# Chunked delta attention and two Mlps on one core: weights signed by ScalarE's Prelu and read where they are converted, group 0's keys first, each group prepared a stage earlier

## The chip, the core and the metric

The kernel runs on one core of a Trainium2 chip. A core has TensorE (PE, with its weight load shown apart as PEld), VectorE (DVE), ScalarE (ACT), GpSimd (POOL) and SyncE (SP, which here issues nearly all transfers), each with an instruction queue worked off in order, and 16 DMA engines. The metric is device time in microseconds (us) per execution, lower is better.

## The reference

```python
k_n = k / (norm(k) + 1e-6)                       # q, k, v: 4 x 8 heads x 768 steps x 48
for t in range(768):
    y[:, :, t] = q_t @ state                     # state 48 x 48 per head
    state += beta_t * outer(kn_t, v_t - state^T kn_t)
x = y as (3072, 384)
h = x @ w_in; P = a0 + a1 h + a2 h^2 + a3 h^3; Q = 1 + |b0||h| + |b1|h^2
x = (P / (Q + 1e-6)) @ w_out                     # Mlp1, 384 -> 2048 -> 384
h = x @ w2_in; out = (h * tanh(softplus(h))) @ w2_out    # Mlp2
```

The four weight matrices arrive as 64-bit floats, passed as integer words. The rest is fp32.

## The kernel before

**Attention.** 768 steps are 24 chunks of 32 (C); four chunks (GU) are a group of 512 columns, six groups. `norms` takes the squares of the keys (ACT), sums (DVE) and roots. `prepare`, per chunk: scale the keys (POOL, L332), a masked beta (`mb`, POOL, L337), transpose keys and queries on PE (L309), copy them to the slot `kq` (ACT, L313), one gram matmul for both (L321), mask its two parts (DVE, L327). `inverse`, per group: a transpose (L357), 30 elimination steps of two instructions each (L366, L372; on POOL for groups 1 to 5, on DVE for group 0), a transpose back (DVE, L376) and a scaling by beta of 1024 columns into `xt` (POOL, L379). `step`, per chunk: the state applied to the keys (L421), its rest `r` (L427), W, the inverse applied to `r` (L433), `u` (L439), the new state S in two halves of 32 matmuls each (L450, L458), then Y, its copy and the transposed X (L469 to L494), which is the Mlp's input. The swapped keys `kns` (L414, L415) are transfers from SBUF to SBUF that S reads.

**Mlps.** Each works group by group in 16 units of 128 hidden columns. A unit is 9 matmuls of 512 columns up (L641), the activation, and 9 down (L647; 12 of 384 columns in the last group's Mlp2, L656): fp32 is carried as two parts, hi and lo, hence three products. A unit fetches its two weight tiles `win` and `wout` from a DRAM scratch `wd` (L634), into 4 slots.

**Weights.** 64 tiles of 128x384 (2 Mlps, 16 f, 2 sides) are converted from 64-bit to fp32 words: raw words by DMA into one of 3 buffers, magnitude by ACT's Abs (L551; on DVE for 20 tiles, L549), a clamp (L554), shift (L559), sign bits (L564) and low bits (L569) on DVE, hi by ACT (L576), lo by POOL (L579), and a store to `wd` (L592).

**What sets the order.** Everything is added to a `Plan` with the engine, an estimated duration, the buffers read and written, and sometimes a due time. `order` simulates the engines and picks, on each, the ready work with the earliest latest start; that makes the fixed order of every queue. Its estimates only choose the order. `heat` matmuls (L787) fill PE's pauses of the head. The stages after the head are: Mlp1 and Mlp2 of group 0, of 1, of 2, of 3 (the steps of group g+1 beside Mlp2 of g, the preparation of g+2 beside Mlp1 of g+1), then Mlp1 of 4, Mlp1 of 5, Mlp2 of 4, Mlp2 of 5.

## Time and profile before

| | |
|---|---|
| median of 3 runs | 1348.69 us (1339.13 to 1351.46) |
| profiled execution, its span | 1342.18 us, 1340.5 us |
| PE, PEld busy | 1098.8 (82%), 873.9 (65%) |
| DVE, ACT, POOL busy | 713.5 (53%), 586.1 (44%), 570.8 (43%) |
| moved by DMA | 224.79 MB, mean 168 GB/s |
| first up matmul of each stage | 113.3, 264.6, 409.6, 500.8, 597.5, 685.2, 786.4, 879.4, 983.0, 1113.0, 1178.7, 1244.0 |

Busy time is the union of an engine's instructions; PE's ends are modelled. In the stage table (Rows 1) a row is a stretch: its bounds, its length, then for PE, PEld, DVE, ACT and POOL the busy us and number of instructions, the mean clock granted to TensorE as a share of full speed, the busy share of the DMA engines, and GB/s. In a group of instructions the columns are line, engine, operation, output and input with shapes, count, then busy us in all and mean ns, then idle us just before them with what ended it. In a timeline they are start, length, engine, line, operation, and in brackets the idle time before with its releaser.

### The profile page before, as it was taken

The page shows a single profiled execution, that of the slowest core. Times are in us where ns is not written, and L with a number is a line of the kernel's source. Part 1 is how long each engine was busy: PE and PEld are TensorE (multiplying, and loading weights), DVE is VectorE, ACT ScalarE, POOL GpSimd, SP SyncE. Part 2 cuts the span into 40 slices and gives each one's busy share as a digit, 9 for nine tenths or more (in the row PEclk, how much of TensorE's full clock was granted, in tenths as well). Part 3 has the DMA queues.
Part 4 walks back from the last instruction along what each step waited for, and adds up shares of the span by engine and source line. Part 5 has one row for each costly group of instructions (what it writes and reads, how often), then busy time and mean ns, then how long its engine had stood idle before and what let it go on. Part 6 is the DMA issues. An engine that isn't in the chain of part 4 may idle for free.

```text
span 1340.5 us, 32163 instructions
## 1 busy us (share of the span) xinstructions
PE 1098.8 (82%) x13168; PEld 873.9 (65%) x13168; DVE 713.5 (53%) x1172; ACT 586.1 (44%) x1022; POOL 570.8 (43%) x699
## 2 busy tenths in 40 slices
...
GB/s 100 116 164 175 240 255 244 205 237 222 263 284 165 174 188 163 136 144 105 243 171 108 141 142 115 231 165 97 126 127 104 80 125 166 195 194 191 151 194 64
DMA packets 209283, 224.79 MB, mean 168 GB/s; under 512 B 134864, under 2 KB 147664, under 8 KB 209136
## 3 DMA queue, kind: packets, MB, share of 16 engines
...
q8 instruction: 104, 1.70, 0.5%
...
q0 software_dynamic: 256, 0.10, 0.0%
...
## 4 chain that ended last, share of the span: by engine, by line
PE 45%; POOL 10%; DVE 9%; DMA 6%; SPq 6%; ACT 5%; issue 3%; DVEq 0%; POOLq 0%; ACTq 0%
PE b_h L641 18%; PE b_o L647 17%; SPq L719 4%; POOL xs L372 4%; POOL tmp L366 3%; PE b_t L450 3%; PE b_t L469 2%; DMA wd<-st 2%; DMA win<-wd 2%; DMA raw<-in_moe_w_in_dram 1%; PE b_t L433 1%; PE b_o L656 1%; POOL gh L687 1%; DVE b_r L684 1%; DMA out_dram<-ev 1%
## 5 line engine op out<-in xcount | busy, mean ns | idle before, releaser
L641 PE MATMUL b_h<-x,win 128*128 128x512 f32 x1728 | 461.5, 415 | 79.2 <-DVE ms L680 42.6
L647 PE MATMUL b_o<-gh,wout 128*128 128x512 f32 x1584 | 417.8, 411 | 66.2 <-POOL gh L687 41.4
L641 PEld LDWEIGHTS b_h<-x,win 128*128 128x128 f32 x1728 | 334.6, 198 | 165.0 <-DVE ms L680 50.8
L647 PEld LDWEIGHTS b_o<-gh,wout 128*128 128x128 f32 x1584 | 302.7, 196 | 145.2 <-POOL gh L687 49.2
L689 ACT ACTIVATE gh<-b_h 128x512 fp32r<-128x512 f32 x96 | 57.4, 598 | 272.3 <-PE b_h L641 266.7
L691 DVE TENSOR_TENSOR gh<-mq,gh 128x512 fp32r<-128x512 f32 x96 | 69.5, 728 | 179.9 <-ACT mq L690 177.2
L678 POOL TENSOR_TENSOR mq<-mq,mr 128x512 f32<-128x512 f32 x96 | 125.6, 1308 | 87.6 <-ACT mr L676 80.0
L687 POOL TENSOR_TENSOR gh<-mq,gh 128x512 fp32r<-128x512 f32 x96 | 125.1, 1304 | 65.2 <-ACT gh L686 51.0
L579 POOL TENSOR_TENSOR st<-wm,st 128x384 fp32r<-128x384 f32 x64 | 68.5, 1077 | 119.6 <-ACT st L576 100.2
L337 POOL TENSOR_TENSOR mb<-beta_t,mask 128x256 f32<-128x256 f32 x24 | 16.6, 690 | 241.4 <-DVE lg L327 241.2
L683 DVE SCALAR_TENSOR_TENSOR mq<-mq,b_r 128x512 f32<-128x512 f32 x96 | 65.4, 682 | 59.6 <-ACT b_r L682 57.0
L672 ACT ACTIVATE mq<-b_h 128x512 f32<-128x512 f32 x96 | 57.0, 593 | 90.8 <-PE b_h L641 64.0
L679 DVE TENSOR_TENSOR ms<-ms,b_h 128x512 f32<-128x512 f32 x96 | 65.2, 679 | 47.4 <-ACT ms L677 46.8
L372 POOL TENSOR_TENSOR xs<-xs,tmp 128x30 f32<-128x30 f32 (+9 forms) x150 | 82.0, 547 | 11.8
L670 ACT ACTIVATE mr<-mq,cst 128x512 f32<-128x512 f32 x96 | 69.1, 721 | 29.1 <-POOL mq L678 28.8
L366 POOL TENSOR_TENSOR tmp<-xs 128x30 f32<-128x30 f32 (+9 forms) x150 | 77.6, 518 | 8.6
L677 ACT ACTIVATE ms<-b_h,ab 128x512 f32<-128x512 f32 x96 | 73.9, 770 | 0.6 <-PE b_h L641 0.6
L680 DVE SCALAR_TENSOR_TENSOR ms<-ms,ab,b_h 128x512 f32<-128x512 f32 x96 | 71.2, 742 | 1.7
L684 DVE SCALAR_TENSOR_TENSOR b_r<-ms,ab,b_r 128x512 f32<-128x512 f32 x96 | 71.8, 748 | 0.0
L682 ACT ACTIVATE b_r<-mr 128x512 f32<-128x512 f32 x96 | 57.5, 599 | 28.8 <-DVE mq L685 27.7
L576 ACT CAST st<-wm 128x384 fp32r<-128x384 f32 x64 | 32.3, 509 | 80.4 <-DVE wm L569 48.6
L686 ACT CAST gh<-mq 128x512 fp32r<-128x512 f32 x96 | 58.7, 612 | 19.3 <-DVE mq L685 19.0
(124 smaller groups left out, 1350.0 us busy)
## 6 DMA issues: line engine op xcount, KB each, us to landing
win<-wd SPq DMA_DIRECT2D x192, 384.0 KB
wout<-wd SPq DMA_DIRECT2D x192, 384.0 KB
...
v<-in_v_dram SPq DMA_DIRECT2D x192, 24.0 KB
...
```

The costliest lines, as they stand in the source:

```text
L366: eng.tensor_tensor(out=tv, in0=xs[:, j, j + 1:C].unsqueeze(1).to_broadcast([128, j, n]), in1=xs[:, 0:j, j:j + 1].to_broadcast([128, j, n] ...
L372: eng.tensor_tensor(out=xs[:, 0:j, j + 1:C], in0=xs[:, 0:j, j + 1:C], in1=tv, op=ALU.add)
L579: nc.gpsimd.tensor_tensor(out=st[:, 1], in0=mf, in1=st[:, 0].bitcast(F32), op=ALU.subtract)
L641: nc.tensor.matmul(out=h, lhsT=win[:, a, j], rhs=x[:, c, slab[j]], start=n == 0, stop=n == 8)
L647: nc.tensor.matmul(out=self.banks[f"o{d}"], lhsT=wout[:, a, d], rhs=gh[:, c], start=first and j == 0, stop=last and j == 2,)
L670: act(out=r, in_=q, func=ACTF.Ln, bias=k["c"])
L677: p.add("ACT", 775, lambda: act(out=s, in_=h, func=ACTF.Identity, scale=k["a3"], bias=k["a2"]), [hb], [sb])
L678: p.add("POOL", 1335, lambda: P.tensor_tensor(out=q, in0=q, in1=r, op=ALU.mult), [rb], [qb])
L680: p.add("DVE", 750, lambda: V.scalar_tensor_tensor(out=s, in0=s, scalar=k["a1"], in1=h, op0=ALU.add, op1=ALU.mult), [hb], [sb])
L684: p.add("DVE", 750, lambda: V.scalar_tensor_tensor(out=rp, in0=s, scalar=k["a0"], in1=rp, op0=ALU.add, op1=ALU.mult), [sb], ["r"])
L687: p.add("POOL", 1320, lambda: P.tensor_tensor(out=gh[:, 1], in0=q, in1=gh[:, 0].bitcast(F32), op=ALU.subtract), [qb], [ghb])
L691: p.add("DVE", 755, lambda: V.tensor_tensor(out=gh[:, 1], in0=q, in1=gh[:, 0].bitcast(F32), op=ALU.subtract), [qb], [ghb])
```

## The change

Weights: one clamp with both signs, then Prelu with a negative slope puts the sign in place (tiles of Mlp1, and of f 0 to 3 of Mlp2), or a scale and a maximum (the other 24 tiles); shift and low bits follow. 24 tiles, all in the head, are clamped on POOL and get their lo by two matmuls with the identity and its negative, and a copy; the others are clamped on DVE and get lo by POOL as before. The split is written to the slot of `win` or `wout` (8 slots for group 0, four of them in the space of the later Mlp inputs), and group 0 reads it there, except for units 8 to 11; it is stored to `wd` as before. The raw buffers are five.

Attention: group 0 does keys, inverse and scaling before its queries, its inverse lies in PSUM, its state copies run on ACT. Later three more `kq` slots take the space of the raw words. S is one operation over both halves, `xt` is scaled chunk by chunk. Group g+3 is prepared beside Mlp2 of g and Mlp1 of g+1, and the steps of group 5 run beside Mlp1 of group 4. The planner's own costs change too.

```diff
-EARLY = 6
-RAW = 3
+HEAD = 12
+FETCHED = range(8, 12)
+EARLY = 4
+RAW = 5
 WM = 3
+SWITCH = 150
+NEAR = 20000
+SIGNS = ""
+PACE1 = 6500
...
+    NT, NKN, NQ, NV, NX = 5, 8, 2, 2, 3
+    WIDE = 12
...
+    def slot(self, u):
+        return u % self.NT if u < self.WIDE else (5, 6, 7, 2, 3, 4, 0, 1)[(u - self.WIDE) % 8]
+    def qslot(self, u):
+        return u if u < GU else u % self.NQ
...
+        for u in range(GU):
+            self.load_k(u, nc.sync, (0, 1))
+            self.load_k(u, nc.scalar, (2, 3))
...
+        for what in ("k", "q") if G == 0 else ("kq",):
+            for g in range(GU):
+                self.prepare(p, GU * G + g, what)
+            if "k" in what:
+                self.inverse(p, G)
+            if what == "k":
+                self.finish(p, G)
+                p.add("DVE", 980, lambda: self.nc.vector.memset(self.pair, 0.0), (), ["o0", "o1"])
...
+            on, eng, ns = ("DVE", nc.vector, 480) if u in (0, 2) else ("POOL", nc.gpsimd, 840)
...
+    def solved(self, G):
+        return (self.xs, ["xs"]) if G else (self.pair.rearrange("p (a b) -> p a b", a=C), ["o0", "o1"])
...
+            if G == 0 and j in (1, half):
+                rows = slice(0, half) if j == 1 else slice(half, C)
+                p.add("ACT", 400 if j == 1 else 800, lambda rows=rows: nc.scalar.copy(out=row[:, rows], in_=xs[:, rows]), xb, ["xs"], early=lead(AHEADX, G))
...
+        def scale(g):
+            part = xt[:, g * M:g * M + M]
+            beta = self.beta_t[:, GU * G + g].unsqueeze(2).to_broadcast([128, M, C])
+            return lambda: eng.tensor_tensor(out=part, in0=part, in1=beta, op=ALU.mult)
...
-        def s_mm(c):
-            s_ps = self.banks[bs[c]]
-            def f():
-                for m in range(M):
-                    a, n = divmod(m, 4)
-                    for e in (c, 2 + c):
-                        r = self.srow(e)
-                        rows = slice(32 * e, 32 * e + 32)
-                        nc.tensor.matmul(
-                            out=s_ps[r:r + 64, m * D:(m + 1) * D],
-                            lhsT=kn[rows, 2 * n + r // 64, :] if a == e // 2 else kns[rows, n, :],
-                            rhs=U[rows, m, :], start=True, stop=True,
-                        )
-            return f
+        def s_mm():
+            for m in range(M):
+                a, n = divmod(m, 4)
+                for e in (0, 3, 1, 2):
+                    r = self.srow(e)
+                    rows = slice(32 * e, 32 * e + 32)
+                    nc.tensor.matmul(
+                        out=self.banks[bs[e % 2]][r:r + 64, m * D:(m + 1) * D],
+                        lhsT=kn[rows, 2 * n + r // 64, :] if a == e // 2 else kns[rows, n, :],
+                        rhs=U[rows, m, :], start=G > 0, stop=True, skip_group_check=G == 0,
+                    )
+        def s_copy(c):
+            return lambda: nc.scalar.copy(out=T[:, c].rearrange("p m d -> p (m d)"), in_=self.banks[bs[c]][:, 0:M * D])
...
+        at, to = (pv, v) if "v" in kind else (v, pv)
...
-        def mag():
-            if late:
-                nc.vector.tensor_scalar(out=m, in0=words[:, :, 1], scalar1=0x7FFFFFFF, scalar2=None, op0=ALU.bitwise_and)
-            else:
-                nc.scalar.activation(out=m.bitcast(F32), in_=words[:, :, 1].bitcast(F32), func=ACTF.Abs)
-        def size():
-            nc.vector.tensor_scalar(
-                out=m.bitcast(F32), in0=m.bitcast(F32), scalar1=self.LEAST, scalar2=self.MOST, op0=ALU.max, op1=ALU.min,
-            )
+        def clamp():
+            (nc.vector if "v" in kind else nc.gpsimd).tensor_scalar(
+                out=at, in0=high.bitcast(F32), scalar1=self.MOST, scalar2=-self.MOST, op0=ALU.min, op1=ALU.max,
+            )
+        def fold():
+            nc.scalar.activation(out=at, in_=at, func=ACTF.Prelu, scale=self.DOWN, alpha=self.SIGN)
+        def scale():
+            nc.scalar.activation(out=to, in_=at, func=ACTF.Identity, scale=self.DOWN)
+        def sign():
+            nc.vector.scalar_tensor_tensor(out=pv, in0=at, scalar=self.SIGN * self.DOWN, in1=to, op0=ALU.mult, op1=ALU.max)
         def shift():
             nc.vector.tensor_scalar(
-                out=m, in0=m, scalar1=3, scalar2=0x3FFFFFF8, op0=ALU.logical_shift_left, op1=ALU.bitwise_and,
-            )
-        def sign():
+                out=ps, in0=ps if kind else m, scalar1=3, scalar2=None, op0=ALU.logical_shift_left,
+            )
+        def tail():
             nc.vector.scalar_tensor_tensor(
-                out=m, in0=words[:, :, 1], scalar=-(1 << 30), in1=m, op0=ALU.bitwise_and, op1=ALU.bitwise_or,
-            )
-        def low():
-            nc.vector.scalar_tensor_tensor(
-                out=m, in0=words[:, :, 0], scalar=29, in1=m, op0=ALU.logical_shift_right, op1=ALU.bitwise_or,
+                out=m, in0=low, scalar=29, in1=ps, op0=ALU.logical_shift_right, op1=ALU.bitwise_or,
             )
...
-            nc.scalar.copy(out=st[:, 0], in_=mf)
+            nc.scalar.copy(out=split[:, 0], in_=mf)
...
+        rest = self.banks["h1"][:, 0:384]
+        def lo_mm():
+            nc.tensor.matmul(out=rest, lhsT=self.ident, rhs=v, start=True, stop=False)
+            nc.tensor.matmul(out=rest, lhsT=self.minus, rhs=split[:, 0].rearrange("p k c -> p (k c)"), start=False, stop=True)
+        def lo_copy():
+            nc.scalar.copy(out=split[:, 1].rearrange("p k c -> p (k c)"), in_=rest)
...
+        here, there = (bank, mb) if "v" in kind else (mb, bank)
+        if "v" in kind:
+            p.add("DVE", 520, clamp, [rawb], [here])
+        else:
+            p.add("POOL", 1490, clamp, [rawb], [here])
         if late:
-            p.add("DVE", 400, mag, [rawb], [mb])
+            p.add("ACT", 550, scale, [here], [there])
+            p.add("DVE", 580, sign, [mb], [bank])
+            p.add("DVE", 470, shift, (), [bank])
         else:
-            p.add("ACT", 550, mag, [rawb, "table"], [mb])
-        p.add("DVE", 400, size, (), [mb])
-        p.add("DVE", 430, shift, (), [mb])
-        p.add("DVE", 640, sign, [rawb], [mb])
-        p.add("DVE", 640, low, [rawb], [mb])
-        p.add("ACT", 510, hi, [mb], [stb])
-        p.add("POOL", 1060, lo, [mb], [stb])
-        p.dma(380, 384, lambda: nc.sync.dma_start(out=self.scratch[f][:, side], in_=st.bitcast(F32)), [stb], [f"wd{self.n}_{f}_{side}"])
+            p.add("ACT", 550, fold, ["table"], [here])
+            p.add("DVE", 470, shift, [here], [bank])
+        p.add("DVE", 550, tail, [rawb, bank], [mb])
+        p.add("ACT", 510, hi, [mb], [buf])
+        if "v" not in kind:
+            p.add("PE", 1000, lo_mm, [mb, buf], ["h1"], early=3000)
+            p.add("ACT", 520, lo_copy, ["h1"], [buf])
+        else:
+            p.add("POOL", 1060, lo, [mb], [buf])
...
+    def wslot(self, i, nf):
+        NW = self.NW
+        if i < nf:
+            return ((0, 1, 2, 3, 4, 5, 6, 7) * 2)[i]
+        if i < 2 * nf:
+            return ((0, 1, 2, 3, 6, 7) * 3)[i - nf]
+        return i % NW
...
+            if i in FETCHED:
...
+        if G or i in FETCHED:
+            p.dma(330, 384, fetch(0, win), [f"wd{m - 1}_{f}_0"], [winb], early=6000)
+            p.dma(330, 384, fetch(1, wout), [f"wd{m - 1}_{f}_1"], [woutb], early=6000)
...
+    def units(m, g, host, convert=lambda f: None):
+        nonlocal due
         for f in range(NF):
+            convert(f)
+            ml.plan_unit(plan, m, g, NG, f, NF, due)
+            due += (PACE if due > START + NF * PACE1 - 1 else PACE1) + HOST * host
+    def first(f):
+        for n in range(HEAD if f == 0 else 0):
+            ml.convert(plan, 1, n, "r", NF, SIGNS)
+        if 0 <= f - 5 < NF - HEAD:
+            ml.convert(plan, 1, HEAD + f - 5, "t1", NF, SIGNS + "v")
+        if 0 <= f - 12 < EARLY:
+            ml.convert(plan, 2, f - 12, "t1", NF, SIGNS + "v")
+    def second(f):
+        for n in (range(EARLY, 6) if f == 0 else (f + 5,)):
+            if n < NF:
+                ml.convert(plan, 2, n, "r", NF, "mv")
+    def prepare(g):
+        at.norms(plan, g)
+        at.prepares(plan, g)
+    units(1, 0, 0, first)
+    at.prepares(plan, 1)
+    at.finish(plan, 1)
+    at.norms(plan, 2)
+    for g in range(NG - 2):
+        at.steps(plan, g + 1)
+        units(2, g, 1, second if g == 0 else lambda f: None)
+        if g == 0:
+            at.prepares(plan, 2)
+        at.finish(plan, g + 2)
+        if g + 3 < NG:
+            at.norms(plan, g + 3)
+            at.prepares(plan, g + 3)
         else:
+            at.steps(plan, g + 2)
+        units(1, g + 1, g + 2 == NG - 1)
+    units(1, NG - 1, 0)
+    units(2, NG - 2, 0)
+    units(2, NG - 1, 0)
```

Three places in the queues, as they stand in the two programs. First POOL, the end of the elimination of the last group (`xs`, `tmp`), with the products of Mlp1 of group 4 behind it (`mq`, `mr`, `gh`). Before:

```order
L372 TENSOR_TENSOR xs_155<-xs_155,tmp_157 128x29x2
L366 TENSOR_TENSOR tmp_157<-xs_155 128x30
L372 TENSOR_TENSOR xs_155<-xs_155,tmp_157 128x30
L687 TENSOR_TENSOR gh_194<-mq_186,gh_194 128x512
L687 TENSOR_TENSOR gh_195<-mq_187,gh_195 128x512
L379 TENSOR_TENSOR xt_156<-xt_156,beta_t_123 128x1024
L674 TENSOR_SCALAR mr_192<-mq_185,ab 128x512
L678 TENSOR_TENSOR mq_185<-mq_185,mr_192 128x512
```

And now:

```order
L425 TENSOR_TENSOR xs_172<-xs_172,tmp_174 128x29x2
L419 TENSOR_TENSOR tmp_174<-xs_172 128x30
L425 TENSOR_TENSOR xs_172<-xs_172,tmp_174 128x30
L449 TENSOR_TENSOR xt_173<-xt_173,beta_t_146 128x256 x4
L798 TENSOR_TENSOR mq_123<-mq_123,mr_132 128x512
L794 TENSOR_SCALAR mr_130<-mq_124,ab 128x512
```

The products `gh` of Mlp1 no longer stand between the elimination and its scale; the Mlp1 work that comes behind the scale begins with its first product.

Second SP, in the head: raw weights (`raw`, now in `arena`), keys of group 1 (`kn`), the swap of the fourth chunk's keys (`kns`), stores to and fetches from the scratch (`wd`). Before:

```order
L192 DMA kn_125<-in_k_dram 32x8x48 x4
...
L545 DMA raw_111<-in_moe_w_in_dram 48x128
L592 DMA wd_1_61<-st_116 128x768
L534 DMA raw_109<-in_moe_w_out_dram 128x384
L414 DMA kns_137<-kn_127 64x4x48
L415 DMA kns_137<-kn_127 64x4x48
L634 DMA win_177<-wd_1_61 128x768
L634 DMA win_178<-wd_2_62 128x768
```

And now:

```order
L610 DMA arena<-in_moe_w_out_dram 128x384
L229 DMA kn_147<-in_k_dram 32x8x48 x4
L617 DMA arena<-in_moe_w_in_dram 48x2x128 x2
...
L477 DMA kns_153<-kn_147 64x4x48
L478 DMA kns_153<-kn_147 64x4x48
L684 DMA wd_5_65<-x_113 128x768
```

The swap stands behind more raw loads (196 transfers of SP are ahead of its second half), no fetch follows it, and the store is from the place where the unit reads.

Third DVE, in Mlp1 of group 0: conversion between the units' own work (`ms`, `mq`, `b_r`). Before:

```order
L679 TENSOR_TENSOR ms_189<-ms_189,b_h_99 128x512
L554 TENSOR_SCALAR wm_114<-wm_114 128x384
L559 TENSOR_SCALAR wm_114<-wm_114 128x384
L554 TENSOR_SCALAR wm_113<-wm_113 128x384
L559 TENSOR_SCALAR wm_113<-wm_113 128x384
L564 SCALAR_TENSOR_TENSOR wm_113<-raw_110,wm_113 128x384
L569 SCALAR_TENSOR_TENSOR wm_113<-raw_110,wm_113 128x384
L564 SCALAR_TENSOR_TENSOR wm_114<-raw_111,wm_114 128x384
L569 SCALAR_TENSOR_TENSOR wm_114<-raw_111,wm_114 128x384
L683 SCALAR_TENSOR_TENSOR mq_186<-mq_186,b_r 128x512
```

And now:

```order
L624 TENSOR_SCALAR b_t_103<-arena 128x384
L799 TENSOR_TENSOR ms_128<-ms_128,b_h_99 128x512
L800 SCALAR_TENSOR_TENSOR ms_128<-ms_128,ab,b_h_99 128x512
L638 TENSOR_SCALAR b_t_103<-b_t_103 128x384
L643 SCALAR_TENSOR_TENSOR arena<-arena,b_t_103 128x384
L803 SCALAR_TENSOR_TENSOR mq_124<-mq_124,b_r 128x512
```

A tile has three instructions on DVE instead of four or five, and its shift and low bits read PSUM.

## Rows read from the trace of the kernel before

**Rows 1.** The stage table: stretches between first up matmuls, and the head.

```profile
0.00:113.30 113.30, 61.94 (x1760) 54.76 (x1760) 68.87 (x161) 28.63 (x59) 30.77 (x60) 0.74 0.55 129
113.30:264.60 151.30, 97.14 (x571) 69.43 (x568) 133.78 (x198) 83.96 (x154) 92.08 (x92) 0.82 0.76 231
264.60:409.60 145.00, 108.93 (x1742) 83.07 (x1742) 98.73 (x178) 48.71 (x91) 61.59 (x75) 0.87 0.81 252
409.60:500.80 91.20, 79.62 (x443) 62.73 (x443) 62.75 (x96) 61.10 (x99) 70.51 (x85) 0.94 0.61 170
500.80:597.50 96.70, 93.68 (x1602) 73.95 (x1601) 26.77 (x42) 27.93 (x53) 14.83 (x25) 0.98 0.57 145
...
983.00:1113.00 130.00, 98.82 (x1737) 76.13 (x1736) 66.30 (x102) 63.01 (x104) 78.59 (x103) 0.88 0.39 105
1113.00:1178.70 65.70, 65.52 (x289) 53.95 (x288) 53.09 (x80) 52.71 (x89) 43.33 (x38) 1.00 0.69 188
...
1244.00:1340.50 96.50, 76.25 (x364) 67.87 (x362) 14.31 (x21) 18.47 (x34) 0.00 (x0) 0.92 0.47 134
```

**Rows 2.** SP's timeline from the start; first and last of 101 issues.

```profile
0.81 4.59 SPq L192 DMA_DIRECT2D kn<-in_k_dram  x8
...
56.96 0.43 SPq L634 DMA_DIRECT2D wout<-wd  x1
```

**Rows 3.** TensorE's timeline at its three longest pauses after 409.6 us.

```profile
713.24 1.50 PE L433 MATMUL b_t<-r,xt 32*32 32x48 f32 x64 [6.90 <-POOL xt L379]
...
907.20 1.50 PE L433 MATMUL b_t<-r,xt 32*32 32x48 f32 x64 [6.68 <-POOL xt L379]
...
1046.47 6.19 PE L647 MATMUL b_o<-gh,wout 128*128 128x512 f32 x16 [27.00 <-POOL gh L687]
```

**Rows 4.** Groups of instructions by form: conversion of weights, POOL's one-input operation.

```profile
L579 POOL TENSOR_TENSOR st<-wm,st 128x384 fp32r<-128x384 f32 x64 | 68.5, 1077 | 119.6 <-ACT st L576 100.2 <-ACT nrm L279 14.8 <-issue 3.7
...
L569 DVE SCALAR_TENSOR_TENSOR wm<-raw,wm 128x384 int32<-128x384 int32 x64 | 47.5, 748 | 1.6
...
L674 POOL TENSOR_SCALAR mr<-mq,ab 128x512 f32<-128x512 f32 x48 | 38.3, 797 | 32.4 <-ACT mq L672 32.3
L554 DVE TENSOR_SCALAR wm<-wm 128x384 f32<-128x384 f32 x64 | 36.5, 570 | 19.7 <-ACT wm L551 18.9
L559 DVE TENSOR_SCALAR wm<-wm 128x384 int32<-128x384 int32 x64 | 32.5, 507 | 2.0
...
L549 DVE TENSOR_SCALAR wm<-raw 128x384 int32<-128x384 int32 x20 | 10.2, 512 | 13.4 <-DMA raw<-in_moe_w_in_dram 6.6 <-POOL st L579 4.2 <-DMA raw<-in_moe_w_out_dram 2.6
```

**Rows 5.** The page's costliest groups: elimination on POOL, five groups.

```profile
L372 POOL TENSOR_TENSOR xs<-xs,tmp 128x30 f32<-128x30 f32 (+9 forms) x150 | 82.0, 547 | 11.8
...
L366 POOL TENSOR_TENSOR tmp<-xs 128x30 f32<-128x30 f32 (+9 forms) x150 | 77.6, 518 | 8.6
```

**Rows 6.** The timeline of all engines, 61 to 68 us.

```profile
61.38 2.01 DVE L376 STREAM_TRANSPOSE xt<-xs 128x1024 f32<-128x1024 f32 x1
...
63.47 1.91 POOL L379 TENSOR_TENSOR xt<-xt,beta_t 128x1024 f32<-128x1024 f32 x1 [24.41 <-DVE xt L376]
63.59 2.00 DVE L554 TENSOR_SCALAR wm<-wm 128x384 f32<-128x384 f32 x1
...
66.61 0.56 DVE L569 SCALAR_TENSOR_TENSOR wm<-raw,wm 128x384 int32<-128x384 int32 x1
```

**Rows 7.** TensorE's timeline, 521 to 530 us: W, a unit, half an S.

```profile
521.85 0.88 PE L433 MATMUL b_t<-r,xt 32*32 32x48 f32 x64
522.66 2.35 PE L641 MATMUL b_h<-x,win 128*128 128x512 f32 x9
524.94 0.25 PE L450 MATMUL b_t<-u,kn 32*64 32x48 f32 x1
...
526.01 2.35 PE L647 MATMUL b_o<-gh,wout 128*128 128x512 f32 x9
```

**Rows 8.** SP's waits: engine, line, waited for, us in total, times, longest.

```profile
SPq L592 <- POOL st L579: 20.7, 14, 6.8
```

More of the change, by code (lines that the diff above doesn't have):

```diff
@@ L104, in order @@
             end = t + self.ops[i][1]
+            if engine == "PE":
+                wide = self.ops[i][1] > 2000
+                end += SWITCH if wide and not was else 0
+                was = wide
             free[engine] = end
@@ L112, in order, with run @@
         return done
-    def run(self, idle, unit, until):
+    def run(self, idle, unit):
         last, fill = None, True
@@ L119, in run @@
             if engine == "PE":
-                fill = fill and i < until
+                fill = fill and ns <= 2000
                 if last is not None and fill:
@@ L185, in bank, with load_k @@
         if u < GU:
-            of = {"t": ("t1", "h0", "h1"), "c": ("t0",), "s": ("o0", "o1"), "y": ("o2",), "x": ("h1",)}[what]
+            of = {"t": ("t1", "h0"), "c": ("t0",), "s": ("o0", "o1"), "y": ("o2",), "x": ("t1",)}[what]
             return of[n % len(of)]
-        return "t1" if what in "tx" else "t0"
-    def load_k(self, u, engine=None):
-        for e in range(4):
+        if u < 2 * GU and what == "t":
+            return "t0"
+        return "t1" if what in "tx" or what == "s" and n else "t0"
+    def load_k(self, u, engine=None, es=range(4)):
+        for e in es:
             (engine or self.nc.sync).dma_start(
@@ new lines, in prepare @@
+        if "q" in what:
+            p.dma(4 * 450, 300, lambda: self.load_q(u), (), [qnb], early=lead(AHEADP, G))
+            p.add("PE", 600, transpose(qn, tq), [qnb], [tq], early=lead(AHEADP, G))
+            p.add("ACT", 580, copy(tq, 1), [tq], [qb] + taken, early=lead(AHEADX, G))
+        p.add("PE", 1100, gram, [kb] + ([qb] if "q" in what else []), [tg], early=lead(AHEADP, G))
+        if "k" in what:
+            p.add("DVE", 430, part(self.lg[:, g], 0, mb), [tg, mbb], [f"lg{g}"], early=lead(AHEADX, G))
@@ L352, in inverse @@
+        if "q" in what:
+            mask_a = self.mask_a.unsqueeze(1).to_broadcast([128, M, C])
+            p.add("DVE", 430, part(am, 1, mask_a), [tg], [ab] + taken, early=lead(AHEADX, G))
+    def solved(self, G):
+        return (self.xs, ["xs"]) if G else (self.pair.rearrange("p (a b) -> p a b", a=C), ["o0", "o1"])
     def inverse(self, p, G):
-        nc, M, tmp, xt, xs = self.nc, self.M, self.tmp, self.xt, self.xs
+        nc, tmp = self.nc, self.tmp
+        xs, xb = self.solved(G)
+        row, half = self.xs, 8
@@ L522, in __init__, with plan @@
+    SIGN = -(2.0 ** 32)
+    def __init__(self, nc, n, w_in, w_out, raw, wm, banks, scratch):
+        self.nc, self.n, self.scratch = nc, n, scratch
+        self.raw, self.wm, self.banks = raw, wm, banks
         self.w_in = w_in
         self.w_out = w_out.rearrange("f (k c) -> f k c", c=128)
-    def plan(self, p, f, side, j, late):
-        nc, bufs = self.nc, self.bufs
-        raw, m, st = (bufs[n][j % len(bufs[n])] for n in ("raw", "wm", "st"))
-        rawb, mb, stb = (f"{n}{j % len(bufs[n])}" for n in ("raw", "wm", "st"))
+    def plan(self, p, f, side, j, bank, split, buf, kind):
+        late = "m" in kind
+        nc = self.nc
+        raw, m = self.raw[j % len(self.raw)], self.wm[j % len(self.wm)]
+        rawb, mb = f"raw{j % len(self.raw)}", f"wm{j % len(self.wm)}"
@@ L615, in __init__, with convert @@
         self.ev = ring("ev", 2, [128, TOK])
-        self.n = 0
+        self.n = self.nst = 0
+    def wslot(self, i, nf):
[5 more added lines that the diff above has]
+        return i % NW
+    def convert(self, p, m, f, bank, nf, kind):
+        i = (m - 1) * nf + f
+        n = self.wslot(i, nf)
+        for side in range(2):
+            split, buf = self.w[side][n], f"w{side}_{n}"
+            if i in FETCHED:
+                g = self.nst % self.NGH
+                self.nst += 1
+                split, buf = self.gh[g].rearrange("p a t -> p (a t)")[:, 0:768].rearrange("p (a k c) -> p a k c", a=2, k=3), f"gh{g}"
+            self.weights[m - 1].plan(p, f, side, 2 * i + side, bank, split, buf, kind)
     def plan_unit(self, p, m, G, NG, f, nf, due):
@@ L757, in tile_delta_attention_two_mlps @@
     psum = ctx.enter_context(tc.tile_pool(name="psum", bufs=1, space=PSUM))
-    banks = {n: psum.tile([128, TOK], F32, name=f"b_{n}") for n in ("h0", "h1", "o0", "o1", "o2", "r", "t0", "t1")}
+    banks = {n: psum.tile([128, TOK], F32, name=f"b_{n}") for n in ("h0", "h1", "o2", "r", "t0", "t1")}
+    pair = psum.tile([128, 2 * TOK], F32, name="b_o")
+    for n in range(2):
+        banks[f"o{n}"] = pair[:, n * TOK:(n + 1) * TOK]
     ab = const.tile([128, 6], F32, name="ab")
```

261 lines of the change are left out of this document (123 added, 138 removed).

## The prediction

> **What bounds the kernel now.** I read the stage table first: how long each stage lasts and how busy each engine is in it. Where TensorE is idle most, something else sets the pace. Then the costs of single instructions, for whatever paces that stage; then the timelines around the largest pauses of TensorE.
>
> The table [rows 1] has three kinds of stage. The head, 113.3 us, prepares and steps the first attention group; no engine is busy for two thirds of it, but SP issues transfers without a pause: from 0.81 to 57.39 us it issued 101 [rows 2], 0.56 us each. The first two Mlp stages (Mlp1 and Mlp2 of group 0) take 151.3 and 145.0 us although a stage of the same 288 matmuls of 512 columns with all weights ready takes 65.7: there the weights are still being converted. DVE is busy 133.8 of the 151.3 us, 88%; of the second stage 98.7 of 145.0. From 409.6 us on, TensorE is busy 80 to 100% of a stage, and what it loses there are named pauses: 6.90 and 6.68 us for a scaled inverse that POOL had not finished, and 27.00 us in the stage from 983 us, for a product of Mlp1 that stood behind an inverse in POOL's queue [rows 3]. So: transfers, then DVE, then TensorE with three holes.
>
> **The change part by part.**
>
> *Head.* Keys are prepared before queries, the group's inverse and its state copies leave POOL and DVE partly, and weights need no fetch. What sets the end is SP's queue: the fourth key swap, which the last state update of group 0 reads ahead of the first Mlp matmul, is the 197th transfer in SP's new order. Before, the 101 issues had 53.6 us of issuing in them and 56.6 with pauses [rows 2], 0.53 to 0.56 each: 197 make 105 to 111 us after the first 0.8. I take 110 for the first Mlp matmul, with 102 and 118 as ends (landing, and the steps after it), against 113.3. The 24 clamps that POOL takes over are priced by their nearest rows: a one-input operation of 512 columns takes 797 ns, so 0.60 for 384; the two-input one of 384 takes 1.08 [rows 4], and I allow twice that, 2.2. POOL is busy 30.8 of 113.3 us in the head [rows 1], so 24 × 2.2 = 53 still fit; I charge nothing, up to (113.3 − 30.8)/24 = 3.4 us each. The two small matmuls and the ScalarE copy that replace POOL's subtraction fall where TensorE and ScalarE are idle for half the head and more.
>
> The Trainium skill, "GPSIMD Engine Reference", section "4.1 Engine selection", speaks against the clamps' place: it wants an elementwise maximum on VectorE, GpSimd being about twice as slow with two inputs. The rows agree in part (0.80 us there for 512 columns, 0.57 for 384 on DVE), but by its advice the sum would have 24 × 0.57 = 14 us more on DVE, in a stretch in which GpSimd has nothing to do.
>
> *Mlp1 of group 0.* Its DVE work was 133.8 us. Now: 53.1 for the 16 units (the same stage of group 5, which has nothing beside it, [rows 1]); 16 tiles, each a clamp (0.512), a shift (0.507) and a tail (0.748), by the rows of the like operations [rows 4], 28.3; and one group's preparation, 62.8 − 53.1 = 9.7 by the stage from 409.6 us. Sum 91. DVE was 88% busy when it set this pace, so 91/0.88 = **103 us** instead of 151.3. What hides the rest: ScalarE was 84 busy and POOL 92 of 151, both with less to do per tile now. Fetches were 16 pairs through DRAM; 28 of group 0's 32 pairs are gone, so the share of the DMA engines, 0.76 to 0.81, falls.
>
> *Mlp2 of group 0.* DVE: 24 tiles × (0.512 + 0.748 + 0.507 + 0.748) = 60, plus 26.8 for the units and steps (the stage from 500.8 us), 87; at 88% that is 99. The second condition is the chain of group 1: its inverse on POOL now runs in this stage. It costs (82.0 + 77.6)/5 = 31.9 us [rows 5]; 14 subtractions of the weights stand between its steps in POOL's new order, 14 × 1.08 = 15; the transpose before the scale is 2.0 [rows 6]; with 4 for the parts and the first scale that makes 53 us before TensorE can form the first W of group 1. In the new order nine of the 16 units stand before it and seven with the four chunks behind it. A unit pair takes 65.7/16 = 4.1, a chunk among them (96.7 − 65.7)/4 = 7.75, less the 1.3 below: 53 + 7 × 4.1 + 4 × 6.45 = **107 us**, instead of 145.0.
>
> *The state product.* A chunk's S came as two operations with a unit between them. One half held TensorE 526.01 − 524.94 = 1.07 us [rows 7], and 9 matmuls behind a switch take 2.28 instead of 65.7/32 = 2.05, so a switch is 0.23. Now one operation of 32 matmuls goes over four row groups. The nearest such thing is W: 32 matmuls, 0.81 us to the next [rows 7]. Ends: 0.81 (gain 1.33) and 2.14 (none); I take one half's time, 1.07, for all of it, so 1.07 and a switch = 1.3 a chunk.
>
> *From Mlp1 of group 1 on*, before 1340.5 − 409.6 = 930.9 us. Each group is prepared one to two stages earlier (eight key slots instead of five allow it), beside an Mlp2, where POOL was busy 15 to 24 of about 100 us; its inverse of 32 and four scales fit. The three pauses go: −40.6. What is late next is the other operand, r of the chunk, or nothing: no other pause there is over 5 us. S: 15 chunks × 1.3 = −19 (ends 0 and −23). The clock: in the stage with the 27 us pause the granted clock was 0.88, elsewhere 0.94 to 1.00; 0.12 × 103 = 12 at most comes back there, I take 5. Sum −65, **866** (845 to 890). The last stage, 96.5 us with its rows and stores, is untouched. At nothing: four scales for one (same elements), the split of the swaps' order, the fifth raw buffer.
>
> Sum: 110 + 103 + 107 + 866 = 1186, and the 1.7 us that the profiled execution's 1342.18 has outside its span: **1188**. That execution lies 6.5 below the median of the runs shown; the sum stands against it.
>
> **The rivals.**
>
> *Contention goes too (0.22).* DVE's instructions were longer beside POOL: a size operation took 2.00 us from 63.59 while POOL's scale ran from 63.47 to 65.38; the low-word operation took 0.56 alone [rows 6], 0.748 on the mean. Tails read PSUM and one buffer now. If they run as when alone, stages drop to their DVE sums: 103 + 92 + 93, and the rest at 860: 1148, **1150**.
>
> The Trainium skill, "SBUF — State Buffer", section "Who interferes with whom", says that a DVE instruction with two SBUF inputs, or in a two-port mode, and a GpSimd one exclude each other, and that one SBUF input outside such a mode does not. The rows at 63.5 agree: the second waited the first out. By that rule alone, 40 tails lose 0.19 each, 8 us on DVE, and the forecast would be 1180.
>
> *Group 0 stays bound by queues (0.20).* The head does not shrink, and the two stages fill worse than 88%: their DVE work falls from 232.5 to 178 us, and at the occupancy of both before, 232.5/296.3 = 0.78, that is 228. With a head of 120 and a rest of 885: 1233; with a head of 125 and 245 for the stages, 1257; I name **1245**. For it: a tile passes five engines, and all of the first 24 share one PSUM bank. Against: two of the steps through DRAM are gone.
>
> *Slower: SP waits (0.04).* SP is one queue; each of the 64 stores of converted weights waits there for the split, and every key, value and weight load behind it waits too. Before, 14 such waits were 20.7 us, the longest 6.8 [rows 8]. The gain is 154 us, plus 13 for one per cent, so it decides from (154 + 13)/64 = 2.6 us a store; at half the longest, 3.4, it gives 1188 + 218 = **1406**. Against: with five raw buffers a load is further ahead of its user than with three.
>
> *The change does not do what it says (0.02).* If Prelu made ScalarE reload its tables per tile, or DMA share still bound group 0, only the later pauses would go: about **1335**. The new order has one table load ahead of the Prelus.
>
> **How the numbers follow.** The forecast holds 0.52, its own range 1160 to 1220: the head's and the rest's bounds, which will hardly all fall to one side. The whole range reaches to 1135, below the contention case, and to 1255, over most of the queue-bound one. About 1% (13 us) is what a measurement of this kernel can tell from no change: faster holds all but the last two cases, 0.94; same 0.02; slower 0.04.
>
> **What would show it.** Right: the first Mlp matmul near 110 us, Mlp2's first near 213, Mlp1 of group 1 near 320; no pause of TensorE over 5 us for a scaled inverse or a product behind one; 32 S matmuls in about 1.1 us; the last inverse done before Mlp1 of group 4. Wrong: first Mlp matmul after 125; a clamp over 3.4 us; the first W of group 1 later than 60 us into Mlp2 of group 0; SP's waits for splits above 100 us; DVE under 80% busy in Mlp1 of group 0 with TensorE waiting for weights.

## The result and the profile after

The changed kernel takes 1232.82 us (median of 4, 1228.04 to 1236.0), the kernel before 1343.91 in the same comparison: ratio 0.9168, 95% interval 0.9103 to 0.9233. The forecast was 1188; the time lies inside the stated range (1135 to 1255), and outside the forecast's own (1160 to 1220). The profiled execution took 1236.0 us, its span is 1234.3.

The stage table of the changed kernel, columns as in [rows 1]; of the stages after 549.5 us only two are shown.

```profile
0.00:137.10 137.10, 83.77 (x2029) 63.41 (x2029) 71.85 (x167) 51.94 (x117) 30.40 (x66) 0.81 0.59 152
137.10:230.00 92.90, 80.18 (x515) 62.69 (x514) 76.32 (x130) 70.98 (x128) 62.39 (x58) 0.93 0.61 187
230.00:357.90 127.90, 98.52 (x1670) 76.62 (x1669) 90.05 (x158) 59.62 (x115) 67.12 (x98) 0.89 0.69 210
357.90:449.50 91.60, 85.92 (x864) 68.28 (x862) 63.43 (x99) 65.43 (x108) 63.04 (x74) 0.98 0.62 164
449.50:549.50 100.00, 89.88 (x1602) 71.15 (x1599) 33.38 (x51) 32.10 (x57) 63.54 (x112) 0.95 0.53 138
...
896.10:1002.80 106.70, 92.24 (x1537) 72.56 (x1536) 57.83 (x89) 59.58 (x97) 42.19 (x37) 0.92 0.47 129
...
1136.20:1234.30 98.10, 75.34 (x364) 66.60 (x362) 14.13 (x21) 18.55 (x34) 0.00 (x0) 0.92 0.45 132
```

Against the forecast's four terms, in us:

| | before | forecast | after | off by |
|---|---|---|---|---|
| head | 113.3 | 110 | 137.1 | +27.1 |
| Mlp1 of group 0 | 151.3 | 103 | 92.9 | -10.1 |
| Mlp2 of group 0 | 145.0 | 107 | 127.9 | +20.9 |
| the rest | 930.9 | 866 | 876.4 | +10.4 |

The four sum to 48.3, the whole error of the span. The head, which was to become a little shorter, became 24 us longer than before; the reader finds why at its end, in the queues. First TensorE's timeline, from 113 us on (a split of a weight tile is the two matmuls of L658 and the one of L659):

```profile
113.49 1.65 PE L658 MATMUL b_h<-arena,ident 128*128 128x384 f32 x2 [7.08 <-ACT x L662]
...
129.59 1.65 PE L658 MATMUL b_h<-arena,ident 128*128 128x384 f32 x2 [1.99 <-ACT gh L662]
...
134.62 1.65 PE L658 MATMUL b_h<-arena,ident 128*128 128x384 f32 x2
135.49 1.09 PE L659 MATMUL b_h<-gh,minus 128*128 128x384 f32 x1
136.39 1.05 PE L353 MATMUL b_t<-ident,kn 128*128 128x128 f32 x4
137.09 1.20 PE L760 MATMUL b_h<-x,win 128*128 128x512 f32 x2
```

The first up matmul (L760) stands behind the splits of weight tiles, 22 of the 24, not only behind the last S, which ran between the two last of them. Each split needs the bank that ScalarE's copy of the split before empties (L662), and TensorE waited 7.08 and 1.99 us for such copies. ScalarE's timeline says why they were late:

```profile
112.14 0.52 ACT L307 ACTIVATE sq<-kn 128x384 f32<-128x384 f32 x1 [9.39 <-DMA kn<-in_k_dram]
...
127.86 0.52 ACT L307 ACTIVATE sq<-kn 128x384 f32<-128x384 f32 x1 [3.80 <-DMA kn<-in_k_dram]
...
129.07 0.47 ACT L662 CAST gh<-b_h 128x384 fp32r<-128x384 f32 x1
```

From 129.5 us, after its pause, to the end of the head TensorE's granted clock was 0.50, the lower of its two levels (1.2 and 2.4 GHz), and the two matmuls of L658 took 1.65 us there against 0.91 at 124.19. SP's timeline shows when the raw weights of the 22nd tile, the fourth swap of keys, the last keys ahead of the first up matmul and a later tile's raw weights were issued:

```profile
113.35 0.36 SPq L610 DMA_DIRECT2D arena<-in_moe_w_out_dram  x1
...
115.72 0.60 SPq L477 DMA_DIRECT2D kns<-kn  x1
...
123.00 2.98 SPq L229 DMA_DIRECT2D kn<-in_k_dram  x4
...
130.60 0.81 SPq L621 DMA_DIRECT2D arena<-in_moe_w_in_dram  x1
```

In the profile's count these are transfer 190, 195 (its second half is 196), 206 to 209, and 218. And ScalarE's waits, in all (us, times, longest):

```profile
ACT sq L307 <- DMA kn<-in_k_dram: 52.6, 14, 9.4
```

So ScalarE stood at the square of a key that was still in flight; all that comes behind it in its queue (Prelu, the halves of the weights, `u`, `x`, Mish) waited too. Before, the same wait was 10.9 us in 7 times. The three of Mlp2 of group 0, in ScalarE's timeline:

```profile
317.33 0.52 ACT L307 ACTIVATE sq<-kn 128x384 f32<-128x384 f32 x1 [2.93 <-DMA kn<-in_k_dram]
...
334.98 0.52 ACT L307 ACTIVATE sq<-kn 128x384 f32<-128x384 f32 x1 [4.44 <-DMA kn<-in_k_dram]
...
350.73 0.52 ACT L307 ACTIVATE sq<-kn 128x384 f32<-128x384 f32 x1 [3.57 <-DMA kn<-in_k_dram]
```

The chain of waits of the same stretch runs through those loads:

```profile
313.52 3.65 DMA kn<-in_k_dram
...
329.50 5.38 DMA kn<-in_k_dram
...
346.07 4.56 DMA kn<-in_k_dram
```

The conversion's own instructions, grouped by form (line, engine, operation, tiles, count, busy us, mean ns, idle before), answer to [rows 4]:

```profile
L643 DVE SCALAR_TENSOR_TENSOR arena<-arena,b_r 128x384 int32<-128x384 int32 x48 | 26.5, 553 | 2.8 <-DVE b_r L638 0.2
...
L638 DVE TENSOR_SCALAR b_r<-b_r 128x384 int32<-128x384 int32 x24 | 13.6, 566 | 0.8
...
L624 POOL TENSOR_SCALAR arena<-arena 128x384 f32<-128x384 f32 x24 | 12.9, 537 | 93.7 <-PE b_h L658 28.8 <-DMA kn<-in_k_dram 23.9 <-DMA arena<-in_moe_w_in_dram 17.7
```

POOL's clamp took 0.54 us (the bounds were 0.60 to 2.2). The low-bits instruction took 553 ns; its relatives before took 748 and 784. One line's own view gives the least, median and longest duration, in ns. First the sign operation before, then the tail after, for its first 24 tiles and the last 24:

```profile
L564 DVE SCALAR_TENSOR_TENSOR wm<-raw,wm x64: 544/559/1537, 25.5 to 399.6; 128x384 int32<-128x384 int32 x64
```

```profile
L643 DVE SCALAR_TENSOR_TENSOR arena<-arena,b_r x48: 530/554/556, 16.5 to 348.1; 128x384 int32<-128x384 int32 x48
```

Before, the median was already 559 ns, and some took 1537. Now no one of the 48 took longer than 556.

### The profile page after: what moved, and what is told of

Read it like the earlier page. It is cut to its first block, busy times and chain, and to the rows that moved or that the text cites. A ratio compares the mean times of both kernels' runs of the same rounds, so it can differ in the third digit from the quotient of the medians.

```text
span 1234.3 us, 32780 instructions
## 1 busy us (share of the span) xinstructions
PE 1070.5 (87%) x13510; PEld 855.5 (69%) x13510; DVE 654.6 (53%) x1088; ACT 617.3 (50%) x1087; POOL 553.5 (45%) x705
## 4 chain that ended last, share of the span: by engine, by line
PE 54%; SPq 15%; DMA 9%; DVE 7%; POOL 7%; ACT 5%; issue 3%; DVEq 0%; POOLq 0%; ACTq 0%
PE b_h L760 23%; PE b_o L766 20%; SPq L839 7%; DMA kn<-in_k_dram 3%; POOL xs L425 2%; PE b_t L531 2%; POOL tmp L419 2%; SPq L229 2%; PE b_t L510 2%; DMA wout<-wd 1%; PE b_o L775 1%; SPq L617 1%; PE b_t L496 1%; DMA wd<-x 1%; SPq L242 1%
## 5 line engine op out<-in xcount | busy, mean ns | idle before, releaser
L760 PE MATMUL b_h<-x,win 128*128 128x512 f32 x1620 | 416.8, 404 | 32.2 <-DMA win<-wd 14.2
L766 PE MATMUL b_o<-gh,wout 128*128 128x512 f32 x1476 | 378.1, 403 | 18.4 <-DMA wout<-wd 9.6
L760 PEld LDWEIGHTS b_h<-x,win 128*128 128x128 f32 x1620 | 306.7, 193 | 104.1 <-DVE ms L800 15.5
L766 PEld LDWEIGHTS b_o<-gh,wout 128*128 128x128 f32 x1476 | 279.2, 192 | 83.0 <-DMA wout<-wd 9.9
L811 DVE TENSOR_TENSOR gh<-mq,gh 128x512 fp32r<-128x512 f32 x96 | 75.6, 788 | 195.3 <-ACT mq L810 185.1
L792 ACT ACTIVATE mq<-b_h 128x512 f32<-128x512 f32 x96 | 56.8, 592 | 62.3 <-PE b_h L760 60.3
L803 DVE SCALAR_TENSOR_TENSOR mq<-mq,b_r 128x512 f32<-128x512 f32 x96 | 65.6, 683 | 38.1 <-ACT b_r L802 34.7
L419 POOL TENSOR_TENSOR tmp<-xs 128x30 f32<-128x30 f32 (+9 forms) x150 | 79.1, 527 | 10.1
L805 DVE SCALAR_TENSOR_TENSOR mq<-mq,b_r 128x512 f32<-128x512 f32 x96 | 65.8, 685 | 2.6
L794 POOL TENSOR_SCALAR mr<-mq,ab 128x512 f32<-128x512 f32 x48 | 37.1, 772 | 60.1 <-ACT mq L792 60.1
L810 ACT ACTIVATE mq<-b_h 128x512 f32<-128x512 f32 x96 | 56.9, 594 | 2.4 <-PE b_h L760 2.4
```

What stands on the lines that cost most here:

```text
L419: eng.tensor_tensor(out=tv, in0=row[:, j, j + 1:C].unsqueeze(1).to_broadcast([128, j, n]), in1=xs[:, 0:j, j:j + 1].to_broadcast([128, j, n ...
L760: nc.tensor.matmul(out=h, lhsT=win[:, a, j], rhs=x[:, c, slab[j]], start=n == 0, stop=n == 8)
L766: nc.tensor.matmul(out=self.banks[f"o{d}"], lhsT=wout[:, a, d], rhs=gh[:, c], start=first and j == 0, stop=last and j == 2,)
L811: p.add("DVE", 755, lambda: V.tensor_tensor(out=gh[:, 1], in0=q, in1=gh[:, 0].bitcast(F32), op=ALU.subtract), [qb], [ghb])
```

## The experiments

Theory A, after reading these rows: the earlier preparation and the larger head put two things in fixed queues ahead of their data, keys on ScalarE and raw weights on TensorE, and these cost what the forecast missed. (Its second half did not hold up; see e5 and e6.) Rivals: SP is late as a whole, whoever waits; or POOL's inverse sets the stage. Each kernel is the changed one with the edit shown, e10 to e12 on top of an earlier one. After every edit the planner orders all queues anew, so a stage can move by some us without the edit being its direct cause. Each kernel's stage table gives the stages named below (head, Mlp1 and Mlp2 of group 0, the rest).

**e1, keys expected later.**

```diff
             p.dma(4 * 450 if G else 10, 300, (lambda u=u: self.load_k(u)) ...
+            p.ops[-1][4] += 4000 if G else 0
```

> The change with one more line: the planner expects key loads of groups 1 to 5 to land 4 us later, so their squares stand later in ScalarE's queue; nothing else is told to it. Theory A (ScalarE stands in its queue at the square of a key that is still being loaded, 52.6 us in 14 waits in the changed kernel, and x, u and the weights' copies stand behind it): the sum of those waits falls below 20 us and the time from 1232.8 to 1200 to 1215. Rival B (SP's queue is late as a whole, and who waits for it makes no difference): the waits move to other ScalarE lines, the time stays within 8 us. Rival C (the preparation, now later, makes the inverses late): pauses of TensorE for scaled inverses over 5 us come back, the time is 1235 to 1260.

1213.46 us, ratio to before 0.9049 (0.8998 to 0.9100). ScalarE's waits:

```profile
ACT sq L308 <- DMA kn<-in_k_dram: 8.9, 4, 3.6
```

The stages, in the same order as above:

```profile
0.00:132.50 132.50, 82.75 (x2031) 63.24 (x2032) 72.19 (x168) 52.38 (x118) 30.29 (x66) 0.85 0.59 154
132.50:216.40 83.90, 78.22 (x510) 61.63 (x508) 72.76 (x124) 67.42 (x121) 60.73 (x56) 0.96 0.65 198
216.40:335.50 119.10, 97.50 (x1674) 74.49 (x1672) 91.42 (x157) 57.38 (x115) 67.81 (x97) 0.93 0.69 215
```

Theory A holds for the keys: 22.4 us are gone by 335.5 us, and the rest takes 877.6, as without the edit (876.4), although 16 of the 52.6 us of waits lay there. No engine has less to do; work only stands in another order. Its median is the lowest of the study.

**e2, nine key slots.**

```diff
-    NT, NKN, NQ, NV, NX = 5, 8, 2, 2, 3
+    NT, NKN, NQ, NV, NX = 5, 9, 2, 2, 3
```

> The change with nine key slots instead of eight, so that a key's load waits for the state update of nine chunks earlier, about one chunk (15 us in Mlp2 of group 0) sooner. Theory A: the three waits of Mlp2 of group 0 (13.6 us of key loads on its chain) go, and two of about 4 us in each of the later Mlp2 stages: 1210 to 1222, and Mlp2 of group 0 about 115 instead of 128 us. Rival B (SP's queue): the loads are issued no sooner, as raw weights and stores are ahead of them, within 8 us of 1232.8.

1230.4 us: the same. The waits fell only to 31.2 us in 10 times, and Mlp2 of group 0 took 132.9. So it is not the slot, and this part of my theory fell. In Mlp2 of group 0 the four loads were issued from 293.1, 311.3, 328.2 and 345.7 us, against 293.7, 311.0, 327.7 and 344.1 without the edit: no sooner, as rival B said, though the stage began 9 us sooner. That SP's queue is the reason is not shown. Mlp1 of group 0 was 83.8 here as well, which I can't lay to the keys alone.

**e3, S in two halves again.**

```diff
-            p.add("PE", 1000, s_mm, ["U", knb, knsb], bs, early=lead(AHEAD, G))
             for c in range(2):
+                p.add("PE", 1140, s_mm(c), ["U", knb, knsb], [bs[c]], early=lead(AHEAD, G))
...
```

> The change with the state update back in two operations of 32 matmuls over two row groups, as before. If the prediction's price holds (one half and a switch, 1.3 us a chunk, of 15 chunks from Mlp1 of group 1 on and 4 before): 1232.8 + 25 = 1258, 19 of it after Mlp2 of group 0. Rival: the stages are held by other waits as well, and the second half fills pauses: below 1243.

1252.12 us, 19.3 more; the rest 889.4, 13.0 more for 15 chunks, 0.87 each where the forecast said 1.3. In the changed kernel one S holds TensorE from 307.21 to 308.29 us, 1.08, as forecast. The 13.0 is not the price of S alone: ScalarE's waits for keys fell to 23.6 us in 5 times here.

**e4, everything of group 0 through DRAM.**

```diff
-FETCHED = range(8, 12)
+FETCHED = range(0, 32)
```

> The change, but every unit of group 0 fetches its weights from the DRAM scratch (28 more pairs of fetches, 21.5 MB and 56 issues of about 0.5 us on SP). If reading in place carries the gain of the first two stages, they become 20 to 45 us longer together, by SP's 28 us and by the landing of a store (6 to 7 us in the changed kernel's chain) ahead of each fetch: 1253 to 1278. Rival (the gain came from fewer and shorter conversion instructions, the fetches were hidden): within 10 us of 1232.8.

1267.8 us, 35 more: Mlp1 of group 0 112.0 (+19.1), Mlp2 136.7 (+8.8), within the expected range; the DMA share 0.80 in both instead of 0.61 and 0.69. Reading weights where they are converted carries a good part of the gain.

**e5, a head of 10 units; e6, the head's clamps on DVE and lo on POOL.**

```diff
-HEAD = 12
+HEAD = 10
```

> The change with 10 instead of 12 units' weights converted in the head (4 tiles less there; they follow beside Mlp1 of group 0, clamped on DVE). Theory A (what the first Mlp matmul waits for is SP's position of the last raw load whose tile is split on TensorE ahead of it: the 219th transfer in the changed kernel, at 0.60 us each; here the 199th): the first Mlp matmul at 125 instead of 137.1 us; Mlp1 of group 0 gains 4 x 1.67 = 7 us of DVE work and becomes about 100 instead of 92.9; the sum is 4 us shorter or the same. Rival (the chain of group 0's own steps sets the head): the first Mlp matmul within 4 us of 137, the time 5 to 10 us longer.

```diff
-SIGNS = ""
+SIGNS = "v"
```

> The change with the head's 24 clamps on DVE and their lo by POOL, as in the other tiles: no matmul and no copy of ScalarE for a split. If SP's queue sets the head, and TensorE's queue no longer holds the split ahead of the first Mlp matmul, the first Mlp matmul comes where the fourth key swap lets it, at 117 to 122 us instead of 137, and the time is 1215 to 1230. Rival (DVE is short of time: 24 x 0.56 = 13 us more on it, 72 of 137 us busy): no gain in the head, 1233 to 1250.

e5: 1227.7 us, the first up matmul at 125.8 (expected 125), Mlp1 of group 0 98.4. e6: 1230.52 us, the first up matmul at 126.8, Mlp1 96.5. One moves four tiles out of the head, one takes all splits off TensorE, and both give 10 to 11 us in the head (e6 less than the 15 to 20 expected). So the splits in TensorE's queue held the head's end. That they wait there for the last raw weights, as the theory said, does not fit the changed kernel's rows. In DVE's timeline the tile that is split at 134.62 us was done before the 218th transfer was issued at 130.60, and that transfer's tile is one that DVE clamps (L624):

```profile
129.93 0.55 DVE L643 SCALAR_TENSOR_TENSOR arena<-arena,b_r 128x384 int32<-128x384 int32 x1
...
135.84 0.56 DVE L624 TENSOR_SCALAR b_t<-arena 128x384 f32<-128x384 f32 x1
```

e5 hit its 125 us all the same, but it moved the last keys forward with the raw weights (from 123.00 to 109.19 us), so its hit doesn't tell the two apart. A third to a half of the gain comes back as a longer Mlp1; the times of both kernels are not told apart from the changed kernel's. That DVE takes 24 clamps more costs the head nothing.

**e7, the order of preparation before.**

```diff
-        if g == 0:
-            at.prepares(plan, 2)
+        at.prepares(plan, g + 2)
         at.finish(plan, g + 2)
-        if g + 3 < NG:
-            at.norms(plan, g + 3)
-            at.prepares(plan, g + 3)
-        else:
-            at.steps(plan, g + 2)
-        units(1, g + 1, g + 2 == NG - 1)
+        units(1, g + 1, 0)
+        at.norms(plan, g + 3)
```

(for the first three groups; the fourth has both steps ahead of its Mlp2, as before)

> The change with the order of preparation as before: group g+2 prepared beside Mlp1 of g+1, the steps of groups 4 and 5 both beside Mlp2 of group 3. By the prediction's step on the three pauses (40.6 us) the stages from Mlp1 of group 1 on become 30 to 50 us longer, 1263 to 1283. Rival (the earlier preparation pays back in ScalarE's waits for keys what it takes from POOL's queue): Mlp2 of group 0 5 to 12 us shorter, the sum 1235 to 1255.

1257.79 us, 25 more, just below the expected range. The rest takes 908.4, 32.0 more, and the long pause is back, in TensorE's waits:

```profile
PE b_o L766 <- POOL gh L807: 30.8, 9, 26.0
```

ScalarE's waits for keys stay at 50.3 us and Mlp2 of group 0 is 2.8 shorter, so the rival's trade isn't there: it is not the moved stage that makes them.

**e8, the old arithmetic.** Magnitude, clamp, shift, sign and low bits as before, from SBUF; split in place. POOL's 24 clamps go with it.

```diff
...
+            p.add("ACT", 550, mag, [rawb, "table"], [mb])
+        p.add("DVE", 400, size, (), [mb])
+        p.add("DVE", 430, old_shift, (), [mb])
+        p.add("DVE", 640, old_sign, [rawb], [mb])
+        p.add("DVE", 640, old_low, [rawb], [mb])
```

> The change with the arithmetic of before in each tile (magnitude on ScalarE, or on DVE for 24 tiles; clamp, shift, sign, low bits on DVE, all from SBUF), still split in place and as the changed kernel splits it. DVE per tile by the rows of before: 2.61 us instead of 1.11 (head), 1.67 (the 16) or 2.24 (the last 24, 3.12 with the magnitude): 36 us more in the head, 15 in Mlp1 of group 0, 21 in Mlp2. If DVE's work sets the two stages: 1258 to 1280. Rival (the stages are held by queues and landings): below 1245.

1257.75 us, 25 more, at the lower end. Three rows of its stage table:

```profile
0.00:134.00 134.00, 79.36 (x2032) 60.95 (x2033) 85.42 (x205) 50.72 (x110) 15.86 (x38) 0.83 0.60 160
134.00:232.10 98.10, 77.55 (x369) 57.95 (x367) 89.63 (x138) 70.70 (x128) 61.61 (x54) 0.97 0.51 156
232.10:381.20 149.10, 113.12 (x1829) 84.59 (x1829) 114.69 (x203) 51.97 (x97) 78.99 (x106) 0.86 0.62 191
```

The head has 14 us more on DVE (36 were expected) and is not longer; Mlp1 has 13.3 more (15) and is 5.2 longer; Mlp2 has 24.6 more (21) and is 21.2 longer. So DVE's work counts in Mlp2, partly in Mlp1, and not in the head. The two operations with both operands from SBUF take 660 and 627 ns on the mean, and 854 and 682 in Mlp1.

**e9, e1 and e5 together; e10, group 1's inverse on DVE; e11, a head of 8.**

> The change with both repairs: the planner expects keys 4 us later (1213.5 alone) and 10 units' weights in the head (1227.7 alone, its head 11.3 us shorter and Mlp1 of group 0 5.5 longer). If the two act in different places, their gains of 19 and 5 us add: 1204 to 1212, the first Mlp matmul at 120 to 126. Rival (both repair the same wait of the head): no faster than 1213.

e10, on top of e9:

```diff
-ONPOOL = (1, 2, 3, 4, 5)
+ONPOOL = (2, 3, 4, 5)
```

> As e9, with the inverse of group 1 on DVE instead of POOL, where group 0's took 24 us before against 48 on POOL here. If the inverse's end sets Mlp2 of group 0 (the first W came 61 to 63 us after the stage's start, and 56 us of units and chunks follow), the first W comes about 20 us earlier and the stage becomes 100 to 110 instead of 119: 1193 to 1203 in all. Rival (DVE is then the bound: 91 + 24 = 115 us of work in the stage): the stage stays at 115 to 130, the time the same as e9 or up to 10 longer.

e11, on top of e9:

```diff
-HEAD = 10
+HEAD = 8
```

> As e9, with 8 units' weights in the head instead of 10. If SP's position of the last raw load still sets the first Mlp matmul, it comes 10 us earlier still (114), and Mlp1 of group 0, with 4 more tiles, is 6 us longer: as e9 or 4 us faster. Rival (with fewer tiles the chain of group 0's steps is the bound): the first Mlp matmul stays within 4 us of that of e9 and the time is 3 to 8 us longer.

e9: 1215.97 us. The head is 118.2 (e1: 132.5), Mlp1 104.8 (83.9): what the head gives, Mlp1 takes and more. e11: 1218.89, 112.6 and 105.1. So e1, e9 and e11 are not told apart, and the gains don't add: the size of the head shifts work between two stages. In e9 the last S and the swap of keys that it reads come together, in TensorE's timeline:

```profile
116.17 0.25 PE L511 MATMUL b_o<-u,kns 32*64 32x48 f32 x1 [0.17 <-DMA kns<-kn]
```

e10: 1228.4, 12 more than e9. The inverse was to take 24 us on DVE; between its two transposes lie 55 us, in DVE's timeline:

```profile
229.29 1.92 DVE L411 STREAM_TRANSPOSE xs<-lg 128x1024 f32<-128x1024 f32 x1
...
284.43 2.12 DVE L445 STREAM_TRANSPOSE xt<-xs 128x1024 f32<-128x1024 f32 x1
```

It shares DVE with the tiles, and Mlp2 becomes 129.2 instead of 120.9. In this order POOL is the better place for it.

**e12, e1 with group 0's queries issued by ScalarE.**

```diff
-            p.dma(4 * 450, 300, lambda: self.load_q(u), (), [qnb], early=lead(AHEADP, G))
+            p.dma(4 * 450, 300, lambda: self.load_q(u, eng_q), (), [qnb], early=..., engine=at_q)
```

> As e1 (1213.5), with the 16 query loads of group 0 issued by ScalarE's queue at its start instead of by SP. If SP's issue rate sets the head and Mlp1 of group 0 together (216.4 us in e1; SP issues without a longer pause up to the first Mlp matmul), 16 issues of 0.5 to 0.6 us fewer bring the first Mlp matmul from 132.5 to 123 to 126 and the time to 1203 to 1207. Rival (the conversion's engines set the sum of the two, as the trade of head against Mlp1 in e9 suggests): the sum of both stays within 4 us of 216, the time within 5 us of 1213.

1235.93 us, 22 more than e1. ScalarE's timeline says why it tells nothing about SP:

```profile
11.11 9.08 ACTq L235 DMA_DIRECT2D qn<-in_q_dram  x8
20.23 0.52 ACT L308 ACTIVATE sq<-kn 128x384 f32<-128x384 f32 x1 [10.53 <-DMA qn<-in_q_dram]
```

Eight issues held ScalarE 9.08 us ahead of the first square, which starts at 20.23 instead of 9.71 us, and group 0's inverse began 12 us later. With ScalarE late itself, the head's end at 133.9 says nothing of SP; SP's own rate stays untested.

## Why the prediction was off, step by step

**The head's end: the step that failed.** The prediction let the fourth key swap set the end and charged nothing for the splits on TensorE and their copies on ScalarE, as both were idle "for half the head and more" (TensorE was busy 61.94 of 113.3 us, so it was idle for 45%). The swap itself came 6 us late: 196 transfers took 0.59 us each, not 0.53 to 0.56, and its issue ended at 117.0. But it did not set the end. The splits stand in TensorE's in-order queue and their copies in ScalarE's, behind squares of keys that come late. What they cost is not their time but their place: the head's end is 10.3 us earlier without them on TensorE (e6), 11.3 with four tiles fewer (e5), 4.6 with the keys planned later (e1), and 18.9 with the last two together (e9), where the swap is as late as the rest of the chain and the head takes 118.2, at the upper of the prediction's ends.

**Mlp1 of group 0: right way, too little.** 92.9 instead of 103. DVE did 76.3 us of work, not 91, and was 82% busy, not 88%. One part is the contention that I had put into a rival: in this stage before, sign and low bits took 952 and 874 ns on the mean, with the old arithmetic in e8 854 and 682; no tail was slowed here. Another is that only 10 of the 16 tiles' clamps and 12 tails fell into it; five of the tiles came in Mlp2. So the work in the term was too large. The Trainium skill, "SBUF — State Buffer", section "Who interferes with whom", says that a DVE instruction with one SBUF input outside the two-port modes doesn't contend with GpSimd; by the rows above, the trace agrees: 48 tails between 530 and 556 ns, against up to 1537 with two SBUF inputs. I had priced that rule at 8 us on DVE.

**Mlp2 of group 0: two parts.** The first W came 61.4 us after the stage's start (291.36 in TensorE's timeline), not 53: the inverse began 6.0 us into the stage, and why stays open. From there to the stage's end it took 66.5 us, not 54, and most of the 12.5 are the keys: 13.6 us of key loads on the chain, and in e1 this part took 56.3. So a wait was missing, ScalarE's for keys, which no rival priced. The nearest rival, keys that stand behind SP's stores, had other numbers: the stores of converted weights waited 56.3 us in 24 times, against the 100 that I had named. DVE's arithmetic is worth 21 us here (e8).

**From Mlp1 of group 1 on: nearly.** 54.5 instead of 65 gained. The pauses gave 32.0 (e7) of 40.6, S 13.0 of 19 (e3, with other waits mixed in). The three pauses are gone as forecast, but others stand in some of their places, a fetch of weights (8.3 us at most) and a bank still being read (7.2). The last two stages are 3.8 and 1.6 us longer, which I had left out. Two readings of [rows 1] were wrong, though no term rests on them: TensorE was busy 76% and 79% in the stages from 983 and 1244 us, not 80 or more, and the last stage's granted clock was 0.92, not at least 0.94.

**The rivals, and the whole.** The measured time is nearer to the queue-bound rival (1245) than to the forecast, and both of its conditions came: the head did not shrink, and DVE was busy 166.4 of the 220.8 us of the two stages, 75%, where it named 78%. What it lacked is the cause that e1 showed, keys in flight ahead of other work on ScalarE. Of the contention-free rival the mechanism came, as no tail was slowed; that the first Mlp stage took 92.9 where it had 92 is luck, for it had DVE full with 16 tiles. Of the prediction's own signs of being wrong two came, the first Mlp matmul after 125 us and the first W later than 60 us into Mlp2. That the time lies in the stated range is owed to the range's upper end, which was set for the queue-bound rival; Mlp1's 10 us the other way made the miss smaller.
